# Projections of an attention and feed-forward kernel: contraction in pieces of 128 rows with an exchange of row halves, and a head that starts on 256 rows

## The chip, the cores and the metric

The kernel runs on one core of a Trainium2 chip. A core has a matrix engine (TensorE, PE in the profile, its weight loads are PEld), a vector engine (VectorE, DVE), a scalar engine (ScalarE, ACT), GpSimd (POOL) and SyncE (SP), which here only issues transfers. Each engine takes its instructions in order. The metric is device time in microseconds, the median of runs; less is better.

## The reference

All arrays are bf16. `x` is 2048 rows of 448 features; xn is its layer norm. Two branches read xn and are multiplied at the end:

```python
xn = _layernorm(x)                                   # 2048 x 448
# attention: 16 query heads of 256, 8 key and value heads, the last 512 cached positions
q = (xn @ wq) as 16 heads                            # wq 448 x 4096
p = softmax(q @ k.T * 256 ** -0.5)                   # 2048 x 512 for each head
s = concat(p @ v over the heads) @ wo                # wo 4096 x 448
# feed-forward
g = silu((gelu(xn @ w_gate) * (xn @ w_up)) @ w_down) # w_gate, w_up 448 x 1792
out = x + s * g
```

The contraction of the three projections from xn (gate, up and q) is 448 long: seven times 64, or three times 128 and 64 more. The array of TensorE has 128 rows.

## The kernel before

A small recorder (`Rec`, lines 28 to 140) takes every operation with the keys it reads and writes, keeps the order of the program on each engine, and puts semaphore waits where a reader follows a writer on another engine, or a writer follows a reader. It puts none between two operations of TensorE. There is no scheduler: the order in the file is the order on each engine.

The 2048 rows are four chunks c of 512 (`QC`), each of four tiles of 128 rows. Row tile t of chunk 0 is loaded by SP as a transfer of its own (line 253); the weights of gate and up come in four slices of columns (`cuts`, line 256: tiles 0 to 1, 2 to 5, 6 to 9, 10 to 13 of 128 columns), gate in partitions 0 to 63 and up in partitions 64 to 127 of one buffer `wgu` (lines 259 to 262), all on SP's queue, with the rows of chunk 1 behind the second slice, then `wd`, then the rows of chunks 2 and 3.

**Head** (lines 331 to 345). Statistics of the four row tiles on VectorE, their square roots on ScalarE, normalization on VectorE, meanwhile twelve 512-column matmuls on zeros (`warm`, line 342); then TensorE transposes each tile in fourteen 64-wide steps (line 321) into PSUM banks 4 to 7, and ScalarE and VectorE copy the result to `xnT` (lines 327 and 329). For chunks 1 to 3 the normalized tile is written twice by VectorE, side by side, and one transposing transfer on SP makes `xnT` of it (line 358), so that each 64-row piece k stands in both row halves of `xnT`.

**Gate and up** (`gate_up`, line 367, matmuls at line 375). For each of the 14 column tiles f: seven pairs of matmuls with 64 contraction rows and 512 columns. The first of a pair uses the lower half of the array's rows and writes the gate bank, the second the upper half and the up bank; a pair runs side by side:

```python
for k in range(NK):
    for b, lo in ((s, 0), (s + 1, HP)):
        ins = e.matmul(bank(b), lhsT=wgu[lo:lo + HP, k, f * P:(f + 1) * P],
                       rhs=xnT[lo:lo + HP, c, k, :], start=k == 0, stop=k == NK - 1)
```

Three bank pairs (0 to 5) are used in turn. ScalarE takes gelu of the gate bank (line 379) and VectorE multiplies it with the up bank (line 381). After a chunk `down` (line 384, matmuls line 387, banks 6 and 7) contracts the 14 tiles with `wd`. Chunk 3's `down` is not done there: it is kept to fill TensorE's time later.

**Attention.** `q_burst` (line 407, matmuls line 418) makes the queries of several heads in the same pairs, two heads side by side, in bank pairs 0/1 and 2/3 in turn; ScalarE copies each pair of banks out (line 422, 128x1024). The first burst is for 4 heads and uses banks 4/5, 0/1, 2/3, 0/1. Then come 256 score steps, step n = 4i + t being row tile t of head-chunk i (lines 546 to 560). A step has two score matmuls into bank 4 + n % 2 (line 433), the exponential on ScalarE with its sum (line 437), reciprocal and scaling on VectorE (lines 439 and 440), and a transposing transfer by SP into `pT`. The exponentials use ten buffers `pr` in turn. From step 12 on every second step has the value product of an earlier head (four matmuls, line 453, copied out by VectorE, line 459), from step 28 the odd ones also four matmuls of the output projection (line 473). A burst of 4 more heads stands in step 12, bursts of 8 in steps 28, 60 and so on.

The 56 matmuls of chunk 3's `down` are spread over score steps by the table at line 541, row tile by row tile, and stand directly behind the step's scores:

```python
b = (6, 7, 7, 2)[t] if c == NQC - 1 else 6 + t % 2            # line 385
for d, slots in ((0, range(0, 4)), (1, range(4, 12)), (2, range(16, 20)), (3, range(20, 24))):
```

VectorE copies each finished tile out of its bank (line 394, `gy`), behind the reciprocal and the scaling of that step in its order.

## Time and profile before

| what | value |
|---|---|
| median of three runs | 559.6 us (559.35 to 559.84) |
| the profiled execution: its own time, its span | 558.75 us, 557.0 us |
| TensorE busy | 548.7 us, 99% of the span |
| VectorE, ScalarE, GpSimd busy | 58%, 53%, 16% |
| TensorE's first gate and up matmul | 9.28 us after the span's start |
| gate and up, one chunk (98 pairs) | 21.26 us |
| a burst of 8 heads (56 pairs) | 12.19 us |

The page gives busy time by engine, the chain of work that ended last, and groups of instructions by line. Times of single groups come from the timeline, which lists instructions in order of time as start, duration, engine, line, operation, output, input and shapes, with the idle time before and what ended it in brackets. The length of a single 512-column matmul in it (0.38 us) includes the draining of the array, which overlaps the next one; what a matmul costs is read from start to start, or from a long group in the chain.

### The profile page before, as it was taken

To read this page: it belongs to the slowest core of one execution; us is meant where nothing else is said; L and a number is where in the kernel's file an instruction comes from. 1 tells how busy PE (TensorE), PEld (TensorE's weight loads), DVE (VectorE), ACT (ScalarE), POOL (GpSimd) and SP (SyncE) were. 2 spreads that over 40 slices of the span, in tenths; PEclk is the share of its full clock that TensorE was granted. 3 is DMA by queue.
4 is the path that set the end of the run, shared out by engine and by line. 5 is a ranking of instruction groups with operands and counts; after the bars stand their busy time and mean duration, and the time that the engine had idled before them with its cause. 6 is when DMAs were issued, how large, how long until landed. Compare 5 with 4: busy or idle time off the path is not lost.

```text
span 557.0 us, 9857 instructions
## 1 busy us (share of the span) xinstructions
PE 548.7 (99%) x3498; PEld 258.8 (46%) x3532; DVE 324.1 (58%) x835; ACT 296.3 (53%) x673; POOL 89.7 (16%) x125
## 2 busy tenths in 40 slices
PE   8999999999999999999999999999999999999997
PEld 4544444444444444444444444444444444444445
DVE  5727446143462688078728744782688078638774
ACT  4423233247746665655575656556665655565631
POOL 0232323200000121001411110042121002411123
PEclk9999999999999999999999999999999999999999
DMA  8996846932453365245535542445354254634552
GB/s 196 276 177 102 138 102 143 264 110 70 95 87 67 67 96 98 46 94 104 112 81 95 104 86 44 100 92 137 75 96 100 34 95 97 120 88 98 93 95 52
DMA packets 169552, 58.83 MB, mean 106 GB/s; under 512 B 160160, under 2 KB 166432, under 8 KB 169504
## 3 DMA queue, kind: packets, MB, share of 16 engines
q1 hardware_dynamic: 166208, 45.50, 44.3%
q0 software_dynamic: 3152, 12.65, 8.7%
q8 instruction: 28, 0.46, 0.4%
q14 instruction: 20, 0.16, 0.1%
q10 hardware_dynamic: 144, 0.06, 0.0%
HBM read 17.92 MB, written 1.84 MB: 35 GB/s over the span
## 4 chain that ended last, share of the span: by engine, by line
PE 97%; DVE 2%; issue 1%; DMA 0%; ACT 0%
PE ps L453 20%; PE ps L433 20%; PE ps L418 18%; PE ps L473 17%; PE ps L375 15%; PE ps L387 8%; DVE tmp L482 0%; DVE xr L484 0%; DVE stats L293 0%; DMA x<-in_A_x_dram 0%; PE ps L321 0%; ACT xnT L327 0%; DVE mv L294 0%; DVE xn L299 0%; DVE rstd L338 0%
## 5 line engine op out<-in xcount | busy, mean ns | idle before, releaser
L437 ACT ACTIVATE pr<-ps 128x512 bf16<-128x512 f32 x256 | 152.7, 597 | 121.4 <-PE ps L433 117.9
L433 PE MATMUL ps<-kT,qT 128*128 128x512 bf16 x493 | 147.7, 379 | 2.0 <-issue 1.4
L453 PE MATMUL ps<-pT,V 128*128 128x512 bf16 x497 | 129.1, 379 | 0.8
L439 DVE RECIPROCAL rden<-den 128x1 f32<-128x1 f32 x256 | 41.5, 162 | 148.2 <-ACT pr L437 129.8
L473 PE MATMUL ps<-wo,oT 128*128 128x448 bf16 (+1 forms) x536 | 116.2, 344 | 0.0
L440 DVE TENSOR_SCALAR pr<-pr,rden 128x512 bf16<-128x512 bf16 x256 | 108.0, 422 | 9.0
L418 PE MATMUL ps<-xnT,wq 64*128 64x512 bf16 x896 | 98.3, 376 | 0.0
L422 ACT ACTIVATE qT<-ps 128x1024 bf16<-128x1024 f32 x64 | 65.5, 1023 | 40.6 <-PE ps L418 40.6
L375 PE MATMUL ps<-xnT,wgu 64*128 64x512 bf16 x784 | 85.3, 376 | 0.8 <-ACT xnT L327 0.8
L459 DVE CAST oT<-ps 128x512 bf16<-128x512 f32 x124 | 84.5, 682 | 0.7 <-PE ps L453 0.5
L453 PEld LDWEIGHTS ps<-pT,V 128*128 128x128 bf16 x512 | 50.0, 98 | 60.2 <-issue 0.3
L473 PEld LDWEIGHTS ps<-wo,oT 128*128 128x128 bf16 x536 | 52.4, 98 | 51.0
L433 PEld LDWEIGHTS ps<-kT,qT 128*128 128x128 bf16 x512 | 49.1, 98 | 55.8 <-issue 4.5
L381 DVE TENSOR_TENSOR actT<-ps,hb 128x512 bf16<-128x512 f32 x56 | 38.1, 685 | 57.2 <-ACT hb L379 55.3
L418 PEld LDWEIGHTS ps<-xnT,wq 64*128 64x128 bf16 x896 | 43.0, 94 | 54.6 <-DVE acc L494 2.5
L379 ACT ACTIVATE hb<-ps 128x512 bf16<-128x512 f32 x56 | 33.4, 597 | 51.4 <-PE ps L375 51.4
L375 PEld LDWEIGHTS ps<-xnT,wgu 64*128 64x128 bf16 x784 | 39.4, 94 | 46.0 <-issue 1.6
L437 ACT ACTIVATION_READ_ACCUMULATOR pr<-ps 128x1 f32 x256 | 49.8, 195 | 0.0
L387 PE MATMUL ps<-wd,actT 128*128 128x448 bf16 x224 | 46.2, 353 | 0.1
L498 POOL TENSOR_TENSOR tmp<-acc,gy 128x448 f32<-128x448 f32 x16 | 16.5, 1034 | 158.6 <-DVE acc L494 158.6
L513 POOL TENSOR_SCALAR tmp<-tmp 128x448 f32<-128x448 f32 x16 | 9.0, 563 | 187.8 <-ACT tmp L512 187.8
L387 PEld LDWEIGHTS ps<-wd,actT 128*128 128x128 bf16 x224 | 21.7, 98 | 22.2 <-issue 1.3
(43 smaller groups left out, 172.4 us busy)
## 6 DMA issues: line engine op xcount, KB each, us to landing
pT<-pr SPq DMA_TRANSPOSE x256, 2.4
wq<-in_A_wq_dram POOLq DMA_DIRECT2D x14, 256.0 KB, 5.2
wo<-in_A_wo_dram POOLq DMA_DIRECT2D x4, 896.0 KB, 6.6
V<-in_A_v_cache_dram POOLq DMA_DIRECT2D x4, 512.0 KB, 5.0
xr<-in_A_x_dram POOLq DMA_DIRECT2D x4, 448.0 KB, 3.9
wd<-in_B_w_down_dram SPq DMA_DIRECT2D x1, 1568.0 KB, 18.5
wgu<-in_B_w_gate_dram SPq DMA_DIRECT2D x3, 448.0 KB, 9.5
wgu<-in_B_w_up_dram SPq DMA_DIRECT2D x3, 448.0 KB, 11.1
```

What stands on the lines that cost most here:

```text
L375: ins = e.matmul(bank(b), lhsT=wgu[lo:lo + HP, k, f * P:(f + 1) * P], rhs=xnT[lo:lo + HP, c, k, :], start=k == 0, stop=k == NK - 1)
L381: dve(lambda e: e.tensor_tensor(actT[:, f, :], bank(s + 1), hb[:, n % NHB, :], ALU.mult), r=[("ps", s + 1), ("hb", n % NHB)], w=[("actT", f)])
L387: pe(lambda e, f=f: e.matmul(bank(b, D), lhsT=actT[:, f, t * P:(t + 1) * P], rhs=wd[:, f, :], start=f == 0, stop=f == NF - 1), r=[("actT", ...
L418: ins = e.matmul(bank(b), lhsT=wq[lo:lo + HP, k, h0 // 2 + hp, e_ * P:(e_ + 1) * P], rhs=xnT[lo:lo + HP, c, k, :], start=k == 0, stop=k == ...
L422: act(lambda e, e_=e_, s=s, buf=buf: e.activation(buf[:, :, e_, :], psum[:, s * 512:(s + 2) * 512].rearrange("p (a q) -> p a q", a=2), ACT ...
L433: ins = e.matmul(bank(b), lhsT=buf[:, a, k, t * P:(t + 1) * P], rhs=kT[:, g, k, :], start=k == 0, stop=k == NE - 1)
L437: act(lambda e: e.activation(pr[s][:, :], bank(b), ACT.Exp, scale=scale, accum_out=den[:, s:s + 1]), r=[("ps", b)], w=[("pr%d" % s,), ("de ...
L439: dve(lambda e: e.reciprocal(rden[:, s:s + 1], den[:, s:s + 1]), r=[("den", s)], w=[("rden", s)])
L440: dve(lambda e: e.tensor_scalar(pr[s][:, :], pr[s][:, :], rden[:, s:s + 1], None, op0=ALU.mult), r=[("pr%d" % s,), ("rden", s)], w=[("pr%d ...
L453: ins = e.matmul(bank(b), lhsT=V[:, j, g, e_ * P:(e_ + 1) * P], rhs=pT[:, i % NPT, j, :], start=j == 0, stop=j == NJ - 1)
L459: dve(lambda e: e.tensor_copy(dst, bank(b)), r=[("ps", b)], w=[key])
L473: ins = e.matmul(bank(b, D)[:, lo:hi], lhsT=oT[G % 2][:, idx, t * P:(t + 1) * P], rhs=wo[:, h0 * NE + idx, lo:hi], start=idx == 0, stop=id ...
```

## The change

The contraction of 448 is cut into three pieces of 128 rows and a rest of 64. `xnT` holds the three pieces once, and the rest in both row halves. The weights lie in 128 partitions (`wg`, `wu`, `wq`), their last 64 rows in `wgu6` and `wq6`, gate's (the even head's) in the lower half and up's (the odd head's) in the upper.

A column tile is now two operations of TensorE (`two_blocks`). Phase 0 has four pairs: gate with the lower half of pieces 0 to 2 and the rest, up with the upper half of them. Phase 1 has three: the halves exchanged, so that the lower half of the array writes the up bank and the upper half the gate bank. As both halves now add into the same bank, phase 1 waits for its phase 0 by a semaphore of TensorE itself (`hard`). Phase 1 of tile f stands behind phase 0 of tile f + 1. Four bank pairs are used in turn for gate and up, three (0 to 5) for the bursts, four in the first burst.

In the head, the rows of tiles 0 and 1 are loaded first, then the weights of column tile 0, then the rows of tiles 2 and 3, and the weights in slices of 1, 2, 4 and 7 column tiles. After tiles 0 and 1 are normalized and transposed, column tiles 0 to 2 are done for the first 256 rows, with tiles 2 and 3 transposed between them, and then for the other 256. Transposes are 128 wide, in banks 6 and 7. The zero matmuls are 38 of 128 columns, and 4 more. The activation table of gelu is loaded ahead by an instruction on a single column.

For chunks 1 to 3 VectorE normalizes once, ScalarE copies the last 64 columns beside it, and the transposing transfer is 512 instead of 896 wide. `pr` has 12 buffers. The row tiles 2 and 3 of chunk 3's `down` move from steps 16 to 19 and 20 to 23 to steps 12 to 15 and 16 to 19, and tile 3 from bank 2 to bank 3.

```diff
-    def op(self, eng, fn, r=(), w=(), dma=False, after=(), lane=None):
+    def op(self, eng, fn, r=(), w=(), dma=False, after=(), lane=None, hard=()):
...
+        for d in hard:
+            d.inc = d.waited = True
+            o.deps.append(d)
...
-        xnT, _ = sb("xnT", [P, NQC, NK, QC], BF16)
+        xnT, _ = sb("xnT", [P, NQC, KF + 1, QC], BF16)
...
-        wq, _ = sb("wq", [P, NK, Hkv, Dh], BF16)
+
+        wq, _ = sb("wq", [P, KF, Hq, Dh], BF16)
+        wq6, _ = sb("wq6", [P, Hq // 2, Dh], BF16)
...
-        wgu, x_at = sb("wgu", [P, NK, F], BF16)
+
+        wg, _ = sb("wg", [P, KF, F], BF16)
+        wu, _ = sb("wu", [P, KF, F], BF16)
+        wgu6, x_at = sb("wgu6", [P, F], BF16)
...
-        xn2, d_at = sb("xn2", [P, NX, NK, 2, HP], BF16)
+        xn2, d_at = sb("xn2", [P, NX, D + HP], BF16)
...
-            while at + 2 * W <= end:
+            while at + 2 * W <= end and len(pr) < 12:
...
-        x0 = [dma("sync", x4[:, t, :], x_view[:, 0, t, :], w=[("x4", t)]) for t in range(TPC)]
+        def load_x0(a, b):
+            dma("sync", x4[:, a:b, :], x_view[:, 0, a:b, :], w=[("x4", t) for t in range(a, b)])
+
...
+        cuts = [0, 1, 3, 7, NF]
...
+            for w, name, src, _ in w_gu:
+                dma("sync", w[:, :, a:b], src[:, :, a:b], w=[(name, s)])
...
+        def load_gu6(a, b):
+
+            for h, (_, name, _, src) in enumerate(w_gu):
+                dma("sync", wgu6[h * HP:(h + 1) * HP, a * P:b * P], src[:, a * P:b * P], w=[("wgu6", h, a > 0)])
...
-        for sl in range(4):
-            load_gu(sl)
-            if sl == 1:
-                load_x(1)
+        for t in range(2):
+            load_x0(t, t + 1)
+        load_gu(0)
+        load_gu6(0, 3)
+        load_x0(2, TPC)
+        load_gu(1)
+        load_gu6(3, NF)
+        load_gu(2)
+        load_x(1)
+        load_gu(3)
...
-        def ln_norm(t, copies=2):
-            s = t % NX
-            for o in range(copies):
-                dve(lambda e, o=o: e.tensor_scalar(
-                    xn2[:, s, :, o, :], x4[:, t, :].rearrange("p (k d) -> p k d", k=NK), mv[:, t, 0:1],
-                    rstd[:, t:t + 1], op0=ALU.subtract, op1=ALU.mult),
-                    r=[("x4", t), ("mv", t), ("rstd", t)], w=[("xn2", s, o)])
+        def ln_norm(t):
+            dve(lambda e: e.tensor_scalar(xn2[:, t % NX, 0:D], x4[:, t, :], mv[:, t, 0:1], rstd[:, t:t + 1],
+                                          op0=ALU.subtract, op1=ALU.mult),
...
-                    ins = e.matmul(bank(3), lhsT=actT[:, NF - 1, 0:P], rhs=actT[:, NF - 1, :], start=True, stop=True)
+                    ins = e.matmul(bank(3, P), lhsT=actT[:, NF - 1, 0:P], rhs=actT[:, NF - 1, 0:P], start=True, stop=True)
...
+            b = 6 + t % 2
+            tp = bank(b).bitcast(BF16)
+
+            def tr(e):
+                for k in range(KF):
+                    e.transpose(tp[:, k * P:(k + 1) * P], xn2[:, t, k * P:(k + 1) * P], ident[:, :])
+                for lo in (0, HP):
+                    ins = e.transpose(tp[lo:lo + HP, KF * P:(KF + 1) * P], xn2[:, t, KF * P:D], ident[:, :])
+                return ins
+            pe(tr, r=[("xn2", t, 0), ("ident",)], w=[("ps", b)])
...
+        def ln_copy(t):
+            b = 6 + t % 2
+            dst = xnT[:, 0, :, t * P:(t + 1) * P]
+            src = bank(b).bitcast(BF16)[:, 0:(KF + 1) * P].rearrange("p (k q) -> p k q", q=P)
+            if t % 2:
+                dve(lambda e: e.tensor_copy(dst, src), r=[("ps", b)], w=[("xnT", 0, t)])
+            else:
+                act(lambda e: e.activation(dst, src, ACT.Copy), r=[("ps", b)], w=[("xnT", 0, t)])
...
+        def ln_first(t):
+            dve(lambda e: e.reciprocal(rstd[:, t:t + 1], std[:, t:t + 1]), r=[("std", t)], w=[("rstd", t)])
+            ln_norm(t)
...
+        warm(38)
+        for t in range(2):
             ln_stats(t)
-            if t % 2:
+            ln_std(t)
+        for t in range(2):
+            ln_first(t)
+            ln_tr(t)
+        warm(4)
+        ln_copy(0)
+        ln_stats(2)
+        ln_copy(1)
+        ln_std(2)
+        ln_stats(3)
+        ln_std(3)
+        act(lambda e: e.activation(small[:, 3:4], small[:, 0:1], ACT.Gelu_apprx_tanh), r=[("eps",)], w=[("warm2",)])
+        for t in range(2, TPC):
+            ln_first(t)
...
+            act(lambda e: e.activation(xn2[:, t % NX, D:D + HP], xn2[:, t % NX, D - HP:D], ACT.Copy),
+                r=[("xn2", t % NX, 0)], w=[("xn2", t % NX, D)])
+            dmaT(xnT[:, c, :, t4 * P:(t4 + 1) * P], xn2[:, t % NX, :],
+                 r=[("xn2", t % NX, 0), ("xn2", t % NX, D)], w=[("xnT", c, t4)])
...
+        phase0 = {}
+
+        def two_blocks(ph, c, s, w, w6, keys, q0=0, q1=QC):
+
+
+            def run(e):
+                for k in range(KF + 1 - ph):
+                    for lo in (0, HP):
+                        m = (lo > 0) ^ ph
+                        lhsT = w[m][lo:lo + HP, k, :] if k < KF else w6[lo:lo + HP, :]
+                        ins = e.matmul(bank(s + m)[:, q0:q1], lhsT=lhsT, rhs=xnT[lo:lo + HP, c, k, q0:q1],
+                                       start=ph == 0 and k == 0, stop=ph == 1 and k == KF - 1)
+                return ins
+            hard = [phase0[s]] if ph else []
+            phase0[s] = pe(run, r=xn(c)[q0 // P:q1 // P] + keys, w=[("ps", s), ("ps", s + 1)], hard=hard)
...
+        NGB = 4
+
+        def gate_up(c, f, ph, q0=0, q1=QC):
...
+            s, h = 2 * (f % NGB), n % NHB
+            keys = [("wg", jslice[f]), ("wu", jslice[f])] + ([] if ph else [("wgu6", a, f >= 3) for a in range(2)])
+            two_blocks(ph, c, s, [w[:, :, f * P:(f + 1) * P] for w in (wg, wu)], wgu6[:, f * P:(f + 1) * P], keys, q0, q1)
+            if ph == 0 or q1 < QC:
+                return
+            act(lambda e: e.activation(hb[:, h, :], bank(s), ACT.Gelu_apprx_tanh), r=[("ps", s)], w=[("hb", h)])
+            dve(lambda e: e.tensor_tensor(actT[:, f, :], bank(s + 1), hb[:, h, :], ALU.mult),
+                r=[("ps", s + 1), ("hb", h)], w=[("actT", f)])
...
-            b = (6, 7, 7, 2)[t] if c == NQC - 1 else 6 + t % 2
+            b = (6, 7, 7, 3)[t] if c == NQC - 1 else 6 + t % 2
...
+            def part(n, ph):
                 hp, e_ = divmod(n, 2)
-                s = 2 * (n % 2) if i0 else (4, 0, 2, 0)[n]
+                s, h = 2 * (n % 3 if i0 else (n + 2) % 4), h0 + 2 * hp
...
+                two_blocks(ph, c, s, [wq[:, :, h + m, e_ * P:(e_ + 1) * P] for m in range(2)],
+                           wq6[:, h // 2, e_ * P:(e_ + 1) * P], wq_keys)
+                if ph:
+                    act(lambda e: e.activation(
+                        buf[:, :, e_, :], psum[:, s * 512:(s + 2) * 512].rearrange("p (a q) -> p a q", a=2), ACT.Copy),
+                        r=[("ps", s), ("ps", s + 1)], w=[(name, e_)])
+
+            for n in range(heads + 1):
+                if n < heads:
+                    part(n, 0)
+                if n:
+                    part(n - 1, 1)
 
...
+            lead = 6 if c == 0 else 2
+            done = 0
+            if c == 0:
+
+                done = 3
+                for f in range(done + 1):
+                    if f < done:
+                        gate_up(0, f, 0, 0, QC // 2)
+                    if f:
+                        if f > 1:
+                            ln_tr(f)
+                            ln_copy(f)
+                        gate_up(0, f - 1, 1, 0, QC // 2)
+            for f in range(NF + 1):
+                if f < NF:
+                    gate_up(c, f, 0, QC // 2 if f < done else 0)
+                if f:
+                    gate_up(c, f - 1, 1, QC // 2 if f - 1 < done else 0)
+                t = (f - lead) // 2
+                if c + 1 < NQC and t >= 0 and f % 2 == 0:
+                    if 1 <= t <= TPC:
+                        ln_later2((c + 1) * TPC + t - 1)
+                    if t < TPC:
+                        ln_later((c + 1) * TPC + t)
                 if f >= 9 and f % 2:
...
-        for d, slots in ((0, range(0, 4)), (1, range(4, 12)), (2, range(16, 20)), (3, range(20, 24))):
+        for d, slots in ((0, range(0, 4)), (1, range(4, 12)), (2, range(12, 16)), (3, range(16, 20))):
```

## The prediction

> **What bounds the kernel now.** I read the page's first part and the chain first.
>
> ```profile
> span 557.0 us, 9857 instructions
> PE 548.7 (99%) x3498; PEld 258.8 (46%) x3532; DVE 324.1 (58%) x835; ACT 296.3 (53%) x673; POOL 89.7 (16%) x125
> ...
> PE 97%; DVE 2%; issue 1%; DMA 0%; ACT 0%
> ```
>
> TensorE is the bound everywhere, and the others have slack. Its work is not changed: a column tile is seven pairs before and 4 + 3 after. So the change can only win where TensorE idles, and lose where it makes TensorE wait. The chain gives 21.26 us for 98 pairs and 12.19 for 56, 0.217 per pair in both, with no extra at the borders of tiles, where waits for other engines stand. I therefore cost the waits between phases at nothing: before a phase 1, phase 0 of the same tile is seven pairs (1.5 us) back, at the end of a burst three (0.65). Next, the timeline of the head:
>
> ```profile
> 0.73 1.82 SPq L238 DMA_DIRECT2D x<-in_A_x_dram  x4
> 1.18 4.95 PE L308 MATMUL ps<-actT 128*128 128x512 bf16 x12 [1.18 <-DVE actT L244]
> 2.81 0.63 DVE L293 BATCH_NORM_STATS2 stats<-x 128x6 f32<-128x448 bf16 x1 [1.69 <-DMA x<-in_A_x_dram]
> ...
> 5.92 0.92 DVE L299 TENSOR_SCALAR xn<-x,mv,rstd 128x448 bf16<-128x448 bf16 x2
> ...
> 7.79 1.39 DVE L329 COPY xnT<-ps 128x896 bf16<-128x896 bf16 x2
> ...
> 9.07 1.28 ACT L379 ACT_TABLE_LOAD   x1
> 9.28 10.97 PE L375 MATMUL ps<-xnT,wgu 64*128 64x512 bf16 x100 [0.77 <-ACT xnT L327]
> ```
>
> Real work starts at 9.28, when VectorE and ScalarE have copied the last transposes. Three column tiles are done at 9.28 + 21 x 0.217 = 13.84; that is the mark for the head. The third view is the timeline around score steps 11 to 13, where the `down` tiles and the bursts' banks move.
>
> ```profile
> 142.56 0.54 PE L387 MATMUL ps<-wd,actT 128*128 128x448 bf16 x2
> ...
> 143.48 0.16 DVE L439 RECIPROCAL rden<-den 128x1 f32<-128x1 f32 x1 [0.26 <-ACT pr L437]
> 143.57 0.60 ACT L437 ACTIVATE pr<-ps 128x512 bf16<-128x512 f32 x1
> 143.68 0.35 DVE L440 TENSOR_SCALAR pr<-pr,rden 128x512 bf16<-128x512 bf16 x1
> 143.95 0.62 DVE L394 CAST gy<-ps 128x448 bf16<-128x448 f32 x1
> ...
> 150.59 1.02 ACT L422 ACTIVATE qT<-ps 128x1024 bf16<-128x1024 f32 x1 [0.49 <-PE ps L418]
> 150.70 0.81 PE L433 MATMUL ps<-kT,qT 128*128 128x512 bf16 x3 [0.16 <-issue]
> ```
>
> Row tile 1 of the last `down` leaves bank 7 at 143.95 + 0.62 = 144.57, 1.6 us after its last matmul, because the copy stands behind step 11's exponential, reciprocal and scaling. Nobody waits for it before.
>
> **The change part by part.**
>
> *Head, until the first group.* SP issues x0 and x1 (1.82 / 4 = 0.455 each), two weight slices (0.66 apart) and two rests (0.455, as the x row) before the rows of tiles 2 and 3: 0.73 + 0.91 + 1.32 + 0.91 = 3.87. A row tile lands 2.1 us after its issue, so these land at 6.0. VectorE has the statistics of two tiles done at 4.38 as before, two reciprocals and normalizations (5.75 to 6.84 for one and two, 1.09, and 0.15 more) at 5.8, and next in its order are the statistics of tile 2, ahead of the copy of tile 1: 6.0 + 0.62 + 0.22 = 6.85. The copy has 512 elements against 896 in 0.62, so 0.35 to 0.62; I take 0.4. TensorE starts at 7.4, 1.9 earlier.
>
> *Head, the three column tiles.* 42 half-width pairs. Half of 0.217 is 0.109; the 224-column output projections take 4.8 us for 48, or 0.114 at 256 columns. I take 0.112: 4.70 for 42. Two transpose groups stand between: 0.16 for a change from half rows to full ones (the "issue" in the third view), 0.1 back, some 0.3 for five matmuls, together 0.55 each. The second half needs tile 3's copy: transposed 0.34 (three pairs) before phase 1 of tile 2 ends, 0.15 to release, 0.4 of copy, 0.1 to TensorE, so TensorE waits 0.3. Tile 2's copy is on ScalarE behind the early table load, at about 10.7, hidden. Sum: 7.4 + 2.35 + 1.1 + 0.3 + 2.35 = 13.5 against 13.84: **-0.35**.
>
> *Loads.* Column tile 1 needs slice 1, issued at 5.0 to 5.6 and landing near 7.7, wanted at 7.85. Column tile 3 needs 2240 KB. Before, a 448 KB slice into 64 partitions came every 2.3 us (195 KB/us), and `wd` into 128 partitions in 4.5 (348 KB/us). From 2.2 on that is 13.7 by the slow rate and 8.6 by the fast; the big slices go to 128 partitions, so I take near 10, hidden with 3 us to spare. The first slices have lines of 256 bytes, which no load of before shows; between the 512-byte slice (224 KB in 1.2 us) and twice its time, the 192 KB take 1 to 2 us, and the upper end puts every later number 1 us back.
>
> The Trainium skill ("DMA: Bandwidth & Descriptors", Specifications) speaks against these pieces: full rate wants 512 bytes, and below that the engine reads, modifies and writes. By it the upper end holds and the whole sum is about 2.2 instead of 1.2. The row above cannot decide it.
>
> *Bank 7 at step 12.* Row tile 2 now begins in step 12, in bank 7. TensorE gets there after the two scores, at 143.37 (its values start there before), and finds the bank taken until 144.57, plus 0.06 to restart: **+1.26**. Queued behind are step 12's values and the burst; ScalarE and VectorE have nothing else to feed them. At the low end 0.9, if VectorE runs step 11 sooner, at the high end 1.6.
>
> *Burst of step 12.* Its third block is now in banks 4/5, and step 13's scores want bank 5. The third block's phase 1 ends three pairs (0.65) before the burst does; ScalarE starts 0.18 later and takes 1.02, so the bank is free 0.55 after the burst, 0.65 with the restart. Before it was 0.16: **+0.49**. Bursts of eight have their last use of 4/5 in the sixth block, long copied out. In all bursts ScalarE ends its last copy 0.37 later (two copies behind one another), and the next exponential with it; step 31's scores, the next on that bank, come 0.76 after it in the burst at 170, so 0.39 of cover is left and the cost is nothing; without the cover it would be up to 0.37 for each of eight bursts. A bank pair is reused after 1.52 us, and its copy ends 1.2 after its last matmul, as before.
>
> *What the moved tiles save.* After that burst the score group of 152.24 (four matmuls, 0.86) lasted until 153.34, 0.24 too long, waiting for exponentials. With seven `down` matmuls there it goes: **-0.24**.
>
> *Off the path.* One normalization less for each of 12 row tiles (0.50 each on VectorE), 12 small ScalarE copies (ScalarE has 51 us idle before gelus), shorter transposes, two more `pr` buffers (no exponential waited for a transfer): 0. The tail is untouched.
>
> Sum: -0.35 + 1.26 + 0.49 - 0.24 = **+1.2**. The profiled execution's 558.75 becomes 559.95; it lies 0.85 under the median, so **560.8**.
>
> The half-width pairs hang on the weight loads. A load takes 94 ns, a half-width matmul 109; in a full-width pair the next load hides entirely behind the matmul (0.217 in all). If it could not, a pair would be 0.203 and the head 3.8 us longer; I keep that as a rival. The Trainium skill says it outright ("TensorE: Matmul & The Clock Gate", What overlaps and what doesn't): a load overlaps running matmuls only in other row groups. By that rule full-width pairs would take 0.31, which the 0.217 contradicts; so I go by the row.
>
> **The rivals.**
> *Head pays in full* (not slower): tiles 2 and 3 are never waited for, transposes slip in for 0.3, and column tile 3 starts at 12.4. 1.1 better: 559.7. It decides from a start of 13.4 on, where the total falls under 560.7.
> *No wait for bank 7*: the copy out is done before TensorE comes. The order of VectorE speaks against it. 1.26 less: 559.5; with the full head 558.4.
> *The first rows do not go ahead*: late rows or weights, column tile 3 not before 14.8: 562.1. SP's queue of six small issues speaks for it.
> *Half-width work at double cost*: loads not hidden (+3.8), or a slower clock: the twelve zero matmuls took 0.41 each, twice the later 0.216, and 38 quarter-width ones end a microsecond sooner. Up to 564.6.
>
> **How the numbers follow.** Forecast 0.47 (560.2 to 561.4), full head 0.15, no bank wait 0.13, late head 0.13, double cost 0.12. A measurement here tells 0.2% (1.1 us) from no change, so slower begins at 560.7. Slower: 0.28 of the forecast, late head and double cost, 0.53. Faster (under 558.5): 0.08 of the no-wait case. Same: 0.39. The range, 559.2 to 563.2, leaves out most of the double cost and the part of no-wait that is faster.
>
> **What would show it.** Right: column tile 3's first matmul at 13.5; TensorE idle 1.2 us before the third `down` tile, released by VectorE's `gy` copy; 0.6 idle after the burst of step 12; pairs still 0.217. Wrong: pairs at another pace, weights waited for in the first 20 us, or no idle at step 12.

## The result, and the profile after

The changed kernel takes 564.07 us in the median of six runs (562.9 to 565.01), the kernel before beside it 559.4 (558.8 to 559.84). The ratio is 1.0084, with a 95% interval of 1.0071 to 1.0097: 0.8% slower. Forecast was 560.8, slower by 0.2%, with a range to 563.2. The profiled execution took 564.12 us, its span is 562.3, 5.3 longer than before.

The page of the changed kernel, first part and shares of the chain:

```profile
span 562.3 us, 9961 instructions
PE 553.4 (98%) x3568; PEld 263.8 (47%) x3568; DVE 318.5 (57%) x825; ACT 296.4 (53%) x688; POOL 88.0 (16%) x125
...
PE 94%; SPq 2%; DMA 1%; DVE 1%; issue 1%; ACT 0%; DVEq 0%
```

TensorE still bounds nearly everything, but 3% of the chain has left it, and SP's queue and a transfer have come in. The longest pieces of the chain (start, length, engine, line, number of instructions):

```profile
4.98 4.95 DMA wu<-in_B_w_up_dram
10.06 2.53 PE ps L410 x22
14.81 19.09 PE ps L410 x196
33.90 10.70 PE ps L434 x56
44.60 21.26 PE ps L410 x196
...
108.51 27.30 PE ps L410 x252
...
174.86 12.19 PE ps L410 x112
...
487.06 12.19 PE ps L410 x112
```

The marks of the kernel before, from its own chain: the end of chunk 0's gate and up, the first burst, the burst of step 28 and the last one.

```profile
30.60 10.70 PE ps L387 x56
...
126.47 6.04 PE ps L418 x56
...
170.02 12.19 PE ps L418 x112
...
482.22 12.19 PE ps L418 x112
```

Chunk 0's gate and up end at 33.90; before it was 30.60. So the head lost **3.30**, where 0.35 of gain was forecast. From there the kernel runs at the old pace: 21.26 per chunk, 12.19 per burst, and from 33.90 to the end of the first burst (108.51 + 27.30 = 135.81) 101.91 us, before 30.60 to 132.51, the same. From the first burst's end to the burst of step 28 it is 39.05, before 37.51: **+1.54** (forecast +1.51). From there to the last burst 312.20 in both. From the last burst's start (487.06, before 482.22) to the end of the span it is 75.24, before 74.78: **+0.46**. Together 5.30, the whole difference.

The head in the timeline (start, duration, engine, line, operation; in brackets the idle time before and what ended it):

```profile
6.89 0.63 DVE L317 BATCH_NORM_STATS2 stats<-x 128x6 f32<-128x448 bf16 x1 [1.56 <-DMA x<-in_A_x_dram]
...
7.65 0.39 DVE L350 COPY xnT<-ps 128x512 bf16<-128x512 bf16 x1
...
8.14 0.27 PE L410 MATMUL ps<-xnT,wg 64*128 64x256 bf16 x1 [1.32 <-ACT std L355]
...
10.06 0.37 PE L410 MATMUL ps<-xnT,wg 64*128 64x256 bf16 x1 [1.31 <-DMA wu<-in_B_w_up_dram]
...
14.81 0.27 PE L410 MATMUL ps<-xnT,wg 64*128 64x256 bf16 x1 [0.18 <-DVE xnT L350]
```

The rows of tiles 2 and 3 were issued at 3.88, as forecast, and landed 3.0 later. VectorE waits for them with the statistics of tile 2, and behind these stands the copy of tile 1 (7.65 to 8.04) that the first group needs. The bracket at 8.14 names a square root; that one ended 0.02 after the copy, and the group does not read it. After phase 0 of column tile 0 TensorE stops again, for up's slice 1. What follows at 10.06 is slow, and the windows say why (stretch and length; busy time and instructions of PE, PEld, DVE, ACT, POOL; then granted clock, DMA share, GB/s):

```profile
6.50:9.90 3.40, 0.94 (x12) 0.51 (x11) 2.74 (x9) 1.35 (x3) 0.00 (x0) 1.00 0.95 227
9.90:13.30 3.40, 3.24 (x29) 2.21 (x31) 0.00 (x0) 0.72 (x2) 0.00 (x0) 0.50 1.05 318
13.30:16.00 2.70, 2.52 (x39) 1.84 (x41) 0.42 (x1) 0.60 (x1) 0.00 (x0) 0.99 1.04 384
```

In the 3.4 us before the clock fell, which hold the first wait and nearly all of the second, TensorE was busy for 0.94. Then the clock is at half for 3.4 us, in which half-width pairs take 0.21 instead of 0.11.

Step 12 and the burst in it:

```profile
146.23 0.59 PE L482 MATMUL ps<-kT,qT 128*128 128x512 bf16 x2
...
147.24 0.62 DVE L441 CAST gy<-ps 128x448 bf16<-128x448 f32 x1
...
147.92 0.74 PE L434 MATMUL ps<-wd,actT 128*128 128x448 bf16 x3 [1.09 <-DVE gy L441]
...
155.07 1.94 ACT L465 ACTIVATE qT<-ps 128x1024 bf16<-128x1024 f32 x2 [0.49 <-PE ps L410]
...
156.15 0.60 PE L482 MATMUL ps<-kT,qT 128*128 128x512 bf16 x2 [0.47 <-ACT qT L465]
```

The third `down` tile waits for bank 7 until VectorE's copy at 147.24 + 0.62 is done: from 146.23 + 0.43 (two score matmuls) to 147.92, 1.26 us. After the burst the scores wait for ScalarE's copy of banks 4/5 to end (155.07 + 1.02 for the first of the two).

The end of the chain:

```profile
547.07 1.22 SPq L248
...
548.38 2.50 DMA pT<-pr
...
551.02 1.89 PE ps L502 x8
```

The last value products wait for the transposing transfer, 1.31 after the one before it on SP, where two score steps take 2.483. The chain of the kernel before has no piece of SP there.

### The profile page after: what moved, and what is told of

It is laid out like the page before. It is cut to its first block, busy times and chain, and to the rows that moved or that the text cites. A ratio compares the mean times of both kernels' runs of the same rounds, so it can differ in the third digit from the quotient of the medians.

```text
span 562.3 us, 9961 instructions
## 1 busy us (share of the span) xinstructions
PE 553.4 (98%) x3568; PEld 263.8 (47%) x3568; DVE 318.5 (57%) x825; ACT 296.4 (53%) x688; POOL 88.0 (16%) x125
## 4 chain that ended last, share of the span: by engine, by line
PE 94%; SPq 2%; DMA 1%; DVE 1%; issue 1%; ACT 0%; DVEq 0%
PE ps L410 33%; PE ps L482 20%; PE ps L502 19%; PE ps L522 15%; PE ps L434 7%; SPq L248 1%; DMA wu<-in_B_w_up_dram 1%; SPq L245 1%; DVE tmp L531 0%; DMA pT<-pr 0%; DVE xr L533 0%; ACT pr L486 0%; ACT qT L465 0%; DVE pr L489 0%; PE ps L339 0%
## 5 line engine op out<-in xcount | busy, mean ns | idle before, releaser
L482 PE MATMUL ps<-kT,qT 128*128 128x512 bf16 x512 | 151.7, 379 | 0.5 <-ACT qT L465 0.5
L502 PE MATMUL ps<-pT,V 128*128 128x512 bf16 x512 | 131.1, 379 | 0.3 <-DMA pT<-pr 0.3
L410 PE MATMUL ps<-xnT,wg 64*128 64x512 bf16 (+1 forms) x354 | 83.5, 369 | 2.8 <-ACT std L355 1.3
L410 PE MATMUL ps<-xnT,wu 64*128 64x512 bf16 (+1 forms) x354 | 84.3, 369 | 0.0
L410 PEld LDWEIGHTS ps<-xnT,wg 64*128 64x128 bf16 x354 | 33.1, 95 | 21.9 <-issue 3.1
L410 PEld LDWEIGHTS ps<-xnT,wu 64*128 64x128 bf16 x354 | 33.1, 95 | 18.8
```

What stands on the lines that cost most here:

```text
L410: ins = e.matmul(bank(s + m)[:, q0:q1], lhsT=lhsT, rhs=xnT[lo:lo + HP, c, k, q0:q1], start=ph == 0 and k == 0, stop=ph == 1 and k == KF - 1)
L482: ins = e.matmul(bank(b), lhsT=buf[:, a, k, t * P:(t + 1) * P], rhs=kT[:, g, k, :], start=k == 0, stop=k == NE - 1)
L502: ins = e.matmul(bank(b), lhsT=V[:, j, g, e_ * P:(e_ + 1) * P], rhs=pT[:, i % NPT, j, :], start=j == 0, stop=j == NJ - 1)
```

## The experiments

The theory after this reading: the head loses by three separate things, late rows (0.74), late weights (1.3) and, as a consequence of both waits, half the clock (about 1.4); the middle loses 1.26 for bank 7 and about 0.5 for banks 4/5. Rivals: the half-width pairs are slow by themselves, because weight loads are not hidden; the weights are late because the queue is too slow, and not because of the order on it; and the moved `down` tiles only show another wait of the same size. All edits are against the changed kernel. These are the stretches of all profiled executions, in us; the kernels without a median below ran once, in that execution. "Middle" is from the end of the first burst to the burst of step 28, "tail" from the start of the last burst to the end of the span. The stretches between them are the same everywhere.

| kernel | first group | chunk 0 ends | middle | tail | span |
|---|---|---|---|---|---|
| before | 9.28 | 30.60 | 37.51 | 74.78 | 557.0 |
| changed | 8.14 | 33.90 | 39.05 | 75.24 | 562.3 |
| clock kept | 8.05 | 32.45 | 39.05 | 75.69 | 561.3 |
| one slice | 8.78 | 31.63 | 39.05 | 75.11 | 559.9 |
| rows first | 7.92 | 30.77 | 39.04 | 74.87 | 558.8 |
| `down` tiles back | 8.05 | 33.80 | 37.78 | 75.30 | 561.0 |
| other burst banks | 8.00 | 34.44 | 38.50 | 75.25 | 562.3 |
| bank 2 for tile 1 | 8.06 | 34.43 | 37.25 | 75.51 | 561.3 |
| three together | 7.81 | 30.66 | 37.77 | 75.06 | 557.6 |
| head mended | 7.69 | 30.11 | 37.77 | 75.21 | 557.2 |
| whole rows | 9.01 | 31.67 | 37.77 | 74.85 | 558.4 |
| all repairs | 7.33 | 29.89 | 37.24 | 74.85 | 556.1 |

### Clock kept: zero matmuls in the two waits

```diff
-        warm(4)
+        warm(24)
         ln_copy(0)
...
                     if f < done:
                         gate_up(0, f, 0, 0, QC // 2)
+                    if f == 0:
+                        warm(24)
```

> The changed kernel with 20 more zero matmuls ahead of the first gate and up group and 24 behind it, where TensorE idles 1.3 and 1.5 us. If the half-width pairs between 10.1 and 13.2 us take 0.21 us because the clock fell in those waits, they take 0.11 now, and column tile 3 starts about 1.3 us earlier (15.8 instead of 17.1), though the loads come as before. If they are slow for another reason (weight loads not hidden behind half-width matmuls, operands just written), they stay at 0.21 and nothing moves.

The waits stay: the groups start at 8.05 and 10.04. But the clock does too:

```profile
8.60:10.06 1.46, 1.46 (x28) 1.36 (x28) 1.00 (x5) 1.31 (x2) 0.00 (x0) 1.00 0.94 210
10.06:11.00 0.94, 0.94 (x19) 0.84 (x20) 0.00 (x0) 0.47 (x2) 0.00 (x0) 1.00 0.95 275
```

Nineteen matmuls instead of ten in the stretch from 10.06 to 11.00; the pairs take 0.11. The second halves begin at 13.36 instead of 14.81, and chunk 0 ends 1.45 earlier. Half-width pairs are not slow by themselves, the clock made them so, and that cost 1.45. The whole kernel won only 1.0 of it, 0.45 went in the tail.

### Rows first, and three column tiles in the first slice

```diff
-        cuts = [0, 1, 3, 7, NF]
-        jslice = {j: s for s in range(4) for j in range(cuts[s], cuts[s + 1])}
+        cuts = [0, 3, 7, NF]
+        jslice = {j: s for s in range(3) for j in range(cuts[s], cuts[s + 1])}
...
-        for t in range(2):
+        for t in range(TPC):
             load_x0(t, t + 1)
         load_gu(0)
         load_gu6(0, 3)
-        load_x0(2, TPC)
         load_gu(1)
         load_gu6(3, NF)
-        load_gu(2)
         load_x(1)
-        load_gu(3)
+        load_gu(2)
```

> The changed kernel with the four row tiles loaded first, then gate and up for column tiles 0 to 2 in one slice, then their rest. If the order of the loads is what held the head (rows of tiles 2 and 3 behind six small issues, slice 1 landing at 9.9), the first group starts near 7.2 instead of 8.1, no group waits for weights, and with the clock kept column tile 3 starts near 13.2 instead of 17.1: the span falls by 3 to 4 us. If loads of 128 rows come no faster than those of 64 did, the 576 KB land only after 8 us and column tile 3 starts at 15 or later.

```profile
7.92 0.27 PE L408 MATMUL ps<-xnT,wg 64*128 64x256 bf16 x1 [1.02 <-DMA wgu<-in_B_w_up_dram]
...
11.69 0.27 PE L408 MATMUL ps<-xnT,wg 64*128 64x256 bf16 x1 [0.18 <-DVE xnT L348]
```

No wait for rows, none for a second slice, the clock at 1.00. Chunk 0 ends at 30.77, 3.13 earlier than in the changed kernel, and the span is 3.5 shorter; 0.37 of that comes from the tail. So the order and the slicing of the loads, with the clock that fell in the waits, and not the speed of the queue, made nearly the whole of the head's loss. A start at 7.2 was too hopeful: the first group now waits for the rest of up, 48 KB into 64 partitions, issued at 4.21 and landing 3.58 later. Even so the head is 0.17 behind the kernel before: starting on 256 rows does not pay for its two waits (1.02 here, and 0.35 before the second halves) and for its transposes.

### One slice: rows of tiles 2 and 3 stay behind

The same, but the rows of tiles 2 and 3 as the change has them, behind the first slice and the first rests.

```diff
-        cuts = [0, 1, 3, 7, NF]
-        jslice = {j: s for s in range(4) for j in range(cuts[s], cuts[s + 1])}
+        cuts = [0, 3, 7, NF]
+        jslice = {j: s for s in range(3) for j in range(cuts[s], cuts[s + 1])}
...
-        load_gu(2)
         load_x(1)
-        load_gu(3)
+        load_gu(2)
```

> The changed kernel with gate and up for column tiles 0 to 2 in one slice, and the rows of tiles 2 and 3 behind it as in the change. If the wait for the separate slice 1 is what costs most, no group waits for weights, though the rows come about 1 us later (near 8) and the first group starts near 9.2; the clock then falls in that one wait or not, and column tile 3 starts at 15 to 16.5 instead of 17.1. If the place of the rows is what costs most, nothing is won, 17 or later.

```profile
8.78 0.27 PE L409 MATMUL ps<-xnT,wg 64*128 64x256 bf16 x1 [1.77 <-ACT std L354]
```

The rows of tiles 2 and 3 land at 7.5, behind a larger slice, and the first group starts later than in the changed kernel. The second wait is gone, and with it the slow clock: one wait of 1.77 did not lower it here. Chunk 0 ends at 31.63, 2.27 earlier than in the changed kernel: the first group starts 0.64 later, and 2.91 is won behind it, by the second wait and the clock. The other 0.86 of the 3.13 of the experiment before is the place of the rows, by which the first group starts at 8.78 instead of 7.92.

### The `down` tiles back at their old steps

```diff
-        for d, slots in ((0, range(0, 4)), (1, range(4, 12)), (2, range(12, 16)), (3, range(16, 20))):
+        for d, slots in ((0, range(0, 4)), (1, range(4, 12)), (2, range(16, 20)), (3, range(20, 24))):
```

> The changed kernel with row tiles 2 and 3 of the last down back in score steps 16 to 19 and 20 to 23. If the wait for VectorE's copy out of bank 7 is what step 12 costs, the idle of 1.26 us there goes, the wait of some 0.24 us for exponentials behind the burst returns, and the burst of step 28 starts 1.0 us earlier, counted from the first burst. If TensorE had lost that time anyway (to the exponentials, say), the distance between the two bursts stays.

The middle is 37.78, 1.27 less than in the changed kernel and 0.27 more than before. The scores after the burst still wait 0.47 for ScalarE's copy.

### Other burst banks: the four-head burst in another order

The burst of step 12 takes its bank pairs in the order 0/1, 4/5, 2/3, 0/1. The changed kernel has 0/1, 2/3, 4/5, 0/1, the kernel before 0/1, 2/3, 0/1, 2/3; so this is a third order, in which 4/5 are copied out one block earlier.

```diff
-                s, h = 2 * (n % 3 if i0 else (n + 2) % 4), h0 + 2 * hp
+                s, h = ((0, 4, 2, 0)[n] if heads == 4 else 2 * (n % 3)) if i0 else 2 * ((n + 2) % 4), h0 + 2 * hp
```

> The changed kernel with the bank pairs of the four-head burst in step 12 in the order 0/1, 4/5, 2/3, 0/1, so that step 13's scores do not want the pair that was used third. If that bank is the wait, TensorE's start behind the burst moves from 0.65 us to 0.2 us after it, 0.45 less; if the exponentials were next in line, part of it comes back at steps 15 and 16.

```profile
149.99 6.22 PE L410 MATMUL ps<-xnT,wq 64*128 64x512 bf16 x56
156.14 0.61 PE L482 MATMUL ps<-kT,qT 128*128 128x512 bf16 x2
```

The scores follow the burst without a wait, 6.15 from start to start. The middle is 38.50, 0.55 less than in the changed kernel. The span is no shorter, since in this execution the head is 0.54 longer: the half clock lasted 6.8 us instead of 3.4.

### Row tile 1 in bank 2, with the other burst banks

```diff
-            b = (6, 7, 7, 3)[t] if c == NQC - 1 else 6 + t % 2
+            b = (6, 2, 7, 3)[t] if c == NQC - 1 else 6 + t % 2
...
-                s, h = 2 * (n % 3 if i0 else (n + 2) % 4), h0 + 2 * hp
+                s, h = ((0, 4, 2, 0)[n] if heads == 4 else 2 * (n % 3)) if i0 else 2 * ((n + 2) % 4), h0 + 2 * hp
```

> The changed kernel with row tile 1 of the last down in bank 2 instead of bank 7, so that row tile 2, still in steps 12 to 15, finds bank 7 empty, and with the bank order 0/1, 4/5, 2/3, 0/1 in the 4-head burst of step 12. Head as in the changed kernel (chunk 0's gate and up end at 33.9 to 34.5). Stretch from the end of the first burst to the burst of step 28: 39.05 in the changed kernel, 38.50 with the bank order alone, 37.78 with the down tiles back at their old steps. Theory (the wait of 1.26 for bank 7 and the wait behind the burst are separate costs, and the moved tiles by themselves save the 0.24 to 0.27 that the exponentials cost before): 38.50 - 1.26 = 37.24, 0.27 under the kernel before (37.51), and no wait ahead of the down tile in step 12. Rival (the late copy out only uncovers another wait of the same size, say for the exponentials or for VectorE): 37.8 or more.

```profile
146.76 0.59 PE L482 MATMUL ps<-kT,qT 128*128 128x512 bf16 x2
147.19 0.73 PE L434 MATMUL ps<-wd,actT 128*128 128x448 bf16 x3
147.76 1.03 PE L502 MATMUL ps<-pT,V 128*128 128x512 bf16 x4
147.77 0.62 DVE L441 CAST gy<-ps 128x448 bf16<-128x448 f32 x1
```

The copy of tile 1 is as late as ever, but the third `down` tile starts 0.43 behind the scores, with no wait. The middle is 37.25: 1.25 less than with the other burst banks alone, and 0.26 less than before, the gain from the moved tiles by themselves. The rival, another wait of the same size, is out.

Its windows at the head show the clock once more:

```profile
5.40:8.80 3.40, 1.71 (x21) 0.98 (x19) 1.89 (x7) 0.95 (x3) 0.00 (x0) 1.00 0.86 241
8.80:15.60 6.80, 5.78 (x50) 3.46 (x52) 1.28 (x4) 2.32 (x4) 0.00 (x0) 0.50 1.05 343
15.60:17.00 1.40, 1.40 (x30) 1.37 (x28) 0.00 (x0) 0.25 (x1) 0.00 (x0) 0.98 1.05 374
```

Here the clock fell at 8.8, after the first wait of 1.57 and some 0.15 of the second, and stayed at half for 6.8.

### Three together: rows first, `down` tiles back, other burst banks

This is the edits of "rows first", "`down` tiles back" and "other burst banks" in one kernel.

> Rows first, the down tiles back in their old steps, and the burst's bank pairs in the other order, all in one. If the three causes found so far are all of the loss, the span is that of rows-first (558.8) less 1.26 and less 0.45, 557.1, which is the kernel before's 557.0 to 0.3 us. If a further loss stands behind them (phases, twelve pr buffers, the tail), it shows as what is left over.

559.42 us, span 557.6. The head is that of "rows first". The middle is 37.77, no better than with the `down` tiles back alone: at the old steps the bank order wins nothing. So the span misses the 557.1 that was expected by 0.5: 0.45 is this, the tail is 0.19 longer than in "rows first", and the head 0.11 shorter. The middle keeps 0.26 over the kernel before.

### Head mended

Three together, with the first two rests issued from ScalarE's queue and tiles 2 and 3 transposed in one go. A phase 0 of the second halves also waits for the group before it on its banks.

```diff
+        load_gu6(0, 3, "scalar")
         act(lambda e: e.activation(small[:, 2:3], small[:, 0:1], ACT.Sqrt), r=[("eps",)], w=[("warm",)])
...
-            hard = [phase0[s]] if ph else []
+            hard = [phase0[s]] if ph or q0 else []
...
-                        if f > 1:
-                            ln_tr(f)
-                            ln_copy(f)
+                        if f == 2:
+                            for t in (2, 3):
+                                ln_tr(t)
+                                ln_copy(t)
```

> The three together, and the rests of the first slice issued by ScalarE's queue, and the two late transposes side by side behind phase 0 of column tile 2. The first group in rows-first waited until 7.8 us for a rest of 64 lines. If the rests' issue behind six others is the cause, the first group starts near 7.0, column tile 3 near 12.6 (before: 13.8), and the kernel is 1.2 us (0.2%) faster than before. If the 1120 KB ahead of that group are simply not there sooner, the start stays at 7.8, column tile 3 starts at 13.5, and the time is the same as before within 0.1%.

559.38 us in the median of eleven runs (558.49 to 560.55) against 558.79: ratio 1.001, interval 1.0001 to 1.0019. Chunk 0 ends at 30.11, 0.49 earlier than in the kernel before: now the early start pays a little. It starts at 7.69 and not at 7.0. The rests land 2.4 and 2.5 after their issue on the other queue, where they took 3.9 and 3.6 behind the first slice in "rows first", so they no longer hold the group; what released it at 7.69 the profile does not settle. The 0.49 is given back in the middle (0.26) and the tail (0.43).

### Whole rows: without the start on 256 rows

Three together, with all four tiles' statistics first, 50 zero matmuls, transposes in banks 4 to 7, and full-width groups only.

```diff
-        warm(38)
-        for t in range(2):
+        warm(50)
+        for t in range(TPC):
             ln_stats(t)
             ln_std(t)
-        for t in range(2):
+        for t in range(TPC):
             ln_first(t)
             ln_tr(t)
-        warm(4)
-        ln_copy(0)
-        ln_stats(2)
-        ln_copy(1)
-        ln_std(2)
-        ln_stats(3)
-        ln_std(3)
+        for t in range(TPC):
+            ln_copy(t)
...
-                done = 3
-                for f in range(done + 1):
...
+                pass
```

> The three together without the start on 256 rows: all four row tiles are normalized and transposed, and copied before the first full-width group. If pieces of 128 rows alone shorten the head (five transposes for fourteen, copies of 512 elements for 896), the first group starts at 8.9 instead of 9.28 and column tile 3 at 13.4 instead of 13.8: 0.4 us faster than before. If the split into 256 rows pays, this kernel is slower than the mended head by 0.5 us or more.

```profile
14.23 0.37 PE L401 MATMUL ps<-xnT,wg 64*128 64x512 bf16 x1 [1.16 <-DMA wgu<-in_B_w_up_dram]
```

559.23 us in the median of eleven (558.85 to 560.2), ratio 1.0003, interval 0.9986 to 1.0019. The first group starts at 9.01, but column tile 3 waits for up's rest for tiles 3 to 13, 176 KB, issued at 6.53 and landing 7.56 later. Without that wait of about 1.2 chunk 0 would end near 30.5, where the kernel before ends. It is a miss: meant to show what the wide pieces win in a plain head, it does not show it, since the load hides it. It does say something of the start on 256 rows: over the runs "head mended" (559.38) is no faster than this kernel (559.23), though the span of its one profile is 1.2 shorter, so no gain of that start is shown either.

### All repairs

The head of "head mended", the other burst banks, the `down` tiles at the steps of the change, and row tile 1 in bank 2.

> The kernel with the mended head (rows first, first weight slice of three tiles, rests on ScalarE's queue, transposes of tiles 2 and 3 together) and the better bank order, but with the down tiles at steps 12 to 15 and 16 to 19 as the change has them and row tile 1 in bank 2. Against the same head with the down tiles at their old steps (chunk 0 ends 30.11, stretch 37.77, span 557.2, ratio 1.001): if the waits are separate costs, the stretch is 37.24 and the span 556.7, with 0 to 0.4 more or less from the tail; ratio 0.999 to 1.000 of the kernel before. Rival (another wait takes their place): stretch 37.8, ratio 1.001. In no case is it faster by 0.2 per cent: TensorE has 1.7 us of idle time in the head and some tenths in the middle to give.

558.91 us in the median of twelve runs (557.53 to 560.38) against 559.11, ratio 0.9989, interval 0.9973 to 1.0005. The middle is 37.24, as foretold, chunk 0 ends at 29.89, the span of the profiled execution is 556.1. That is 0.9 less than before in one execution, but over the runs no gain is shown. With the waits named here taken away or shortened, the change is worth nothing that this measurement can tell.

## Why the prediction was wrong, step by step

**Head, until the first group: wrong by 0.74.** "These land at 6.0" was a latency of 2.1, read from a row tile alone on an empty queue. Behind two slices and two rests, and for two tiles at once, it was 3.0. The issue time came out right (3.87 against 3.88) by luck: the two weight slices took 0.47 and 0.53 to issue where 0.66 each was put, the two rests 0.61 and 0.63 where 0.455 each was put. The rest of the chain from there, statistics then copy, stood in the prediction.

**Loads: wrong, and the largest error.** Slice 1 was to land "near 7.7", and the upper end was to put "every later number 1 us back". Gate's part landed at 7.4, up's at 9.93. The DMA view of the first 16 us, in slices of 0.4, shows what was missed (busy tenths of the DMA engines, GB/s, and three of the issues with size and time from issue to landing):

```profile
DMA  0000498676727589996799999999999999999999
GB/s 0 0 0 0 81 247 212 171 174 158 113 48 140 98 321 323 288 170 152 176 228 312 280 243 229 157 268 302 311 346 352 402 402 376 390 431 363 372 372 390
...
wg<-in_B_w_gate_dram SPq DMA_DIRECT2D x1, 192.0 KB, 2.9
wu<-in_B_w_up_dram SPq DMA_DIRECT2D x1, 192.0 KB, 5.0
wgu<-in_B_w_gate_dram SPq DMA_DIRECT2D x1, 176.0 KB, 5.4
```

TensorE at 10.06 needed 1120 KB (448 of rows, 192, 96 and 384 of weights), 1.15 MB. The first twenty slices sum to 2872, times 0.4 is 1.15 MB: so much had been moved by 8.0. By 10.0 it was 1.67 MB. So for these bytes the rate was near the estimate (8.0 against 7.7); but half a megabyte that was wanted later, the rests of tiles 3 to 13 and slice 2, had gone in between. (The 2240 KB of column tile 3, put "near 10", had been moved by 12.2, which no group waited for.) The estimate took the transfers to finish in the order of their bytes. That they share the engines instead is the reading that these landings suggest; it was not tried by itself: two equal slices issued 0.47 apart land 2.5 apart, the one with more issued behind it late. Before that, from 4.0 to 5.6, the queue moved only 48 to 140 GB/s, with the engines at 2 tenths in one slice: six small issues in a row, 0.5 to 0.6 apart, seem to have given them too little to do; "rows first", with its 288 KB slices in flight there, moved 325 to 373 GB/s from 4.4 to 5.6.

On the rule that the prediction weighed, full rate only from 512 bytes (the Trainium skill, "DMA: Bandwidth & Descriptors", Specifications), the runs say little: gate's first slice, with lines of 256 bytes, landed 2.2 after its issue, like a row tile of nearly its size (2.1), and slice 1, the one that was waited for, has lines of 512.

**Head, the three column tiles: the mechanism right, the clock missed.** A half-width pair costs 0.11 at the full clock, as taken (0.112), with loads hidden; the second halves run from 14.81 in 2.35, and the wait before them at full clock is 0.35 ("so TensorE waits 0.3"), in "rows first". But the first half lasted 6.67 from its start instead of 3.75 from 7.4 to 11.15: a wait of 1.3, 1.45 for the half clock, and 0.17 left. The two rivals that the prediction held apart, "the first rows do not go ahead" and "a slower clock" under double cost, came together, since the waits of the one caused the other. The reason given for a slower clock, that the zero matmuls end sooner, was not it as it was put: the first group still ran its pairs in 0.11 at 8.14, and the clock fell only at 9.9. What it lacked was work in the waits, as "clock kept" shows.

**Bank 7: right.** Forecast +1.26; 1.26 from start to start in the changed kernel, 1.25 by taking it away.

**Burst of step 12: right in place, 0.49 forecast, 0.55 measured.** From burst to scores it is 6.70 from start to start (149.45 to 156.15), 6.15 without the wait. The forecast came near by two errors that partly cancel: it had 0.65 for the wait, and took off 0.16 that the kernel before was to have lost there. That 0.16 is no wait. The row of 150.70 has three score matmuls where four stand in the program, and the timeline has four weight loads from 150.47 on. Of the kernel before 19 records of score matmuls are missing in the trace, as the counts of its page show:

```profile
L433 PE MATMUL ps<-kT,qT 128*128 128x512 bf16 x493 | 147.7, 379 | 2.0 <-issue 1.4
L433 PEld LDWEIGHTS ps<-kT,qT 128*128 128x128 bf16 x512 | 49.1, 98 | 55.8 <-issue 4.5
```

One of them is the first of these four; with it the scores begin near 150.48, 6.15 behind the burst's start at 144.33. (The prediction took from the same row 0.16 for a change from half rows to full ones; the transpose groups in the head still cost what it put, 0.55 each, in "rows first": 9.56 to 10.12 and 10.46 to 11.01.) And the cost depends on its neighbour: with the `down` tiles at their old steps the middle is 0.27 over the kernel before with the bank wait and 0.26 over it without, so there the wait itself adds nothing, since the exponentials are waited for anyway. What remains, 0.26, comes with the two last copies of ScalarE behind one another: in "three together" the first exponential stands 7.44 behind the burst's start, in the kernel before 7.18. The prediction had that in view for the other bursts ("0.39 of cover is left") and not for this one.

**What the moved tiles save: right.** Forecast -0.24; 37.25 against 37.51, -0.26, once their waits are gone.

**Phases, pairs, work off the path: right.** A chunk takes 21.26 and a burst 12.19 as before; the wait of a phase 1 for its phase 0 costs nothing that shows.

**The tail: "untouched" was wrong by 0.46.** Where SP's transposing transfers stand in the chain at the end, the tail is 75.2 to 75.7; in the kernels where they don't it is 74.8 to 75.1. Apart from the kernel before, all have twelve `pr` buffers, in both kinds, so these alone are not the cause. Why SP's queue is behind in some executions was not tried and stays open. So does the spread of the new versions: the runs of each of the three repaired ones lie 1.4 to 2.9 apart, while of the 21 runs of the kernel before that stand beside two of them nineteen lie within 0.6 (the other two reach 559.93 and 563.78).

In sum: +1.51 in the middle held to 0.03; -0.35 in the head was +3.30; and 0.46 came in a place that had been ruled out.

## What to carry to other kernels

In a head that is bound by loads, count what is wanted first in bytes and put what is wanted later behind it with care: here two equal slices landed 2.5 apart, most likely because later transfers shared the engines with them, and a rate that was near enough for their bytes did not save the forecast. Loading the rows first and the three column tiles in one slice won 3.13. A wait of TensorE early in the kernel is priced with what it does to the clock, here 1.45 on top of two waits of 1.3. And before a tile moves ahead, look up who still holds the bank that it goes to: that price, read off the copy's place in VectorE's order, came out to the hundredth.

## What the runs showed of the hardware

The clock fell without a long wait. In the changed kernel two waits of 1.32 and 1.30 with 0.6 of matmuls between them halved it; in the 3.4 us before it fell TensorE was busy for 0.94 of them. In "bank 2 for tile 1" it was busy for 1.71 of 3.4, just half, and in "other burst banks" for 1.77; there the clock fell 0.15 and 0.06 after the end of the first group, hardly into the second wait, so that one wait of 1.57 or 1.59 had been enough. Yet one wait of 1.77 ("one slice", busy for 1.63 from 6.5 to 9.9) or of 1.16 ("whole rows") left it at full. So no threshold of busy time comes out of these runs.

What the falls have in common is their distance from the rise. The granted clock does not show the rise: it reads 1.00 from the first microsecond on, though 38 zero matmuls of 128 columns took 4.23 there, 0.111 each, and 24 of them at 8.66 in "clock kept" 1.45, 0.06 each. The transposes show it, here the second group of three in the changed kernel and in "other burst banks":

```profile
5.71 0.50 PE L339 MATMUL ps<-ident,xn 128*128 128x128 bf16 x3
...
5.57 0.34 PE L339 MATMUL ps<-ident,xn 128*128 128x128 bf16 x3
```

By such rows the clock rose near 6.5 in the changed kernel, 6.4 in "`down` tiles back", 5.4 in "bank 2 for tile 1" and 5.3 in "other burst banks" (estimates, from the first operations at the new pace), and it fell at 9.9, 9.8, 8.8 and 8.7: 3.4 later each time. It stayed at half for 3.4 us in the first two and for 6.8 in the others, and nothing between. The mean granted clock of the six runs of the changed kernel, 0.997 in four and 0.994 and 0.993 in two, agrees with such spells: 3.4 at half clock make 0.997 of 562, 6.8 make 0.994. The Trainium skill ("TensorE: Matmul & The Clock Gate", What's actually happening) has the clock set by a free-running window of 3.413 us; the lengths agree with one and two such windows. It lets the clock fall after an idle window, and elsewhere on the page (Why this matters for your kernels) advises against gaps over some 3 us; the runs here differ, since no wait reached 1.8. That the same kernel falls early or late by where its waits meet the window is argued from these times, and was not tried.

Small transfers into 64 partitions are slow for their size among others: in "rows first" 48 KB took 3.9 and 3.6 us from issue to landing and 176 KB 5.4 and 5.7, where slices of 384 KB into 128 partitions, issued between them, took 4.0 and 5.3.
